# An attention, soft-mixture and feed-forward kernel: queries loaded with a token's heads side by side, and another order of work inside a step

## The chip, the core and the metric

The kernel runs on one core of a Trainium2 chip. Its engines work side by side, each through its own list of instructions in order: TensorE (PE) multiplies and transposes, VectorE (DVE) and ScalarE (ACT) do element-wise work and carry results out of the accumulator memory PSUM, GpSimd (POOL) works on SBUF alone, and SyncE (SP) issues the DMAs. The metric is the device time of one execution in microseconds (us).

## The reference

```
q_d, k_d, v_d = means of 4 neighbouring tokens of q, k, v
out = repeat(softmax(q_d k_d^T / 8) v_d, 4) + softmax(q k^T / 8 where |i - j| < 4) v
x = heads of out side by side                              # 2304 x 512
logits = x @ phi;  d = softmax over tokens;  c = softmax over slots
slot_out[e] = max((d.T @ x)[e] @ w1[e], 0) @ w2[e]         # 8 experts, 4 slots each
y = c @ slot_out                                           # 2304 x 512
result = max(y @ w_in, 0) ** 2 @ w_out                     # 512 -> 2048 -> 512
```

q, k and v are 4 batches x 8 heads x 576 tokens x 64 numbers in float32. w_in and w_out are float64; the kernel reads them as pairs of int32 and makes float32 of them on DVE ("narrow", L228 to L234, five turns over each piece).

## The kernel before

**Units and steps.** A batch and a pair of heads make a unit; there are 16. A written list, `START`, takes units 0 to 2 through their first stages. A loop over s = 3 to 15 then works through a string, `ORDER`, once per step; every letter is a stage, applied to unit s or to one that began one to five steps earlier, and a list `DRAIN` ends the attention. The scheduler is manual: an engine's instructions stand in the order of these letters.

Of unit s: `T` transposes the queries and `K` the keys (L404; ACT's L410 and L412 and DVE's L412 carry them out of PSUM into `q` and `kz`), `d` sums groups of four tokens on POOL into `qkd` (L420, L422), `Q` issues the loads of q and k of unit s+2 (L372). Of unit s-1: `S` local scores (L428, L434) with a maximum and a subtraction on DVE (L441, L442), `E` their exponential on ACT (L447), `s` coarse scores `sd` (L457), `m` their maximum, `e` their exponential `pd` (L468), `n`, `N` the sums and divisions (`pl` and `pd` on POOL), `L` the load of v (L389). Of s-2: `p` transposes the local probabilities (`ptp`, L495) and ACT copies them to `pt` (L496); `q` does that for the coarse ones (`pdp`, L507; `pdt`, L508). Of s-3: `V` multiplies with the values (`av`, L520), `x` and `X` make the coarse values (`vt`, `vdp`, `vd`). Of s-4: `D` multiplies the coarse ones (L549; ACT's `xd`, L554), `A` adds both (`xt`, L562), `t` transposes to tokens (`xp`, `xrp`; ACT's `xk`, `xr`) and forms the logits (L582). `h`, `H`, `g`, `G` are a batch's soft-mixture work; in the loop they fall in steps 8 and 12. `C` and `c` are narrowing turns, `l` issues weight loads.

**What sets when work can start.** All transposes, keys and queries included, share one PSUM tag `t` with three buffers: the fourth transpose in order waits until the first has been carried out. `pl`, `pt`, `qkd`, `xk` and `xr` have one buffer each; q, k, `kz`, `pdt` and `xt` have two. SP issues its DMAs in order; the eight landing semaphores are used in turn, so a DMA waits for the landing of the one issued eight before it. A plain step issues q, k, four pieces of v and two or three weight pieces.

**After the attention** come the soft-mixture's experts and then the feed-forward part, a loop of 80 hidden products (`up`, L1006), with the output products `po` (L1087) between them. The 2304 tokens come in five chunks. `SLOTS` says beside which of the hidden products the last pieces of the combine stand: `r1`, `r2`, `r3` make slices of a right factor (`arp`, L989; `rows`, L994 on ACT; `ast`, L996 on DVE) and `i2`, `i3` multiply w_in's last column blocks (`ap`, L979). `up`, `ap` and `arp` share one PSUM buffer.

Of the kernel before, what the change touches and what calls it, by code (L numbers as in the profile page):

```python
# [18 lines left out]
B, H, S, D = 4, 8, 576, 64  # L19
NP = H // 2  # L20
NU = B * NP
# [24 lines left out]
W32 = 5  # L46
LBE = 5
LOADN = [2, 2, 3] * 6
ORDER = "DTAhSEsmCHKQdgVxLepGtnXNqlc"
START = "T0 K0 phi L0 Q2 d0 f4 T1 S0 E0 s0 m0 K1 l2 Q3 d1 P e0 n0 N0 T2 S1 E1 s1 m1 K2 L1 Q4 l2 d2 e1 p0 n1 q0 N1 l2"  # L50
DDVE = (2,)
NDVE = (0,)
# [3 lines left out]
NRING = 28  # L56

LPOS = [0, 0, 0, 0, 8, 10, 12, 14, 67, 69, 70, 71, 74, 74, 77, 77]
SLOTS = {3: ['r1'], 11: ['i2'], 13: ['r2'], 19: ['i3'], 21: ['r3']}
NORDER = "w,w w,w w,w w,w o0,o1 o2 w,o3 o4,w o5,w w,o6 o7,w o8,w o9,w w,o10 o11,o12 o13,o14 o15"  # L60
NEXP = {(2, 0): 1, (6, 2): 1, (6, 3): 1, (7, 0): 1, (7, 1): 1}
WRES = 4
# [8 lines left out]
def attention_moe_ffn_kernel(  # L71
# [12 lines left out]
    nc = tc.nc  # L84
# [7 lines left out]
    def bank(tag, shape, bufs, name, dt=F32):  # L92
        return ps.tile(shape, dt, tag=tag, bufs=bufs, name=name)

    def bt(shape, name):
        return bank("t", shape, 3, name)
# [4 lines left out]
    ident = cp.tile([128, 128], F32, name="ident")  # L101
# [5 lines left out]
    for g in range(4):  # L107
        r = slice(32 * g, 32 * g + 32)
# [56 lines left out]
    def load_next(n=1):  # L165
        for _ in range(n):
            if not loads or not free:
                return
            kind, i, j = loads[0]

            fits = [x for x in free if x[0] is not wa or kind in ("w1", "w2") and i == 0 and int(x[1][1:]) >= WRES]
            fits.sort(key=lambda x: x[0] is not wa)
            if kind == "wout" or kind == "win" and (LPOS[4 * j + i] > 50 or lb is None) or kind != "win" and i == NE - 1:
                fits = [x for x in free if x[0] is ring]
            elif kind != "win" and i >= LBE + 1:
                fits = [x for x in fits if x[1][0] != "b"]
                fits.sort(key=lambda x: x[0] is ring)

            if any(j > 1 and (j, i // 2) not in win for k, i, j in got if k == "win") and kind != "win":
                if sum(x[0] is ring for x in free) < 2:  # L180
                    fits = [x for x in fits if x[0] is not ring]
            if not fits:
                return
            place = fits[0]
            free.remove(place)
            loads.popleft()
            load(kind, i, j, place)
# [109 lines left out]
    def narrow_next(n=1):  # L297
        for _ in range(n):
            narrow_turn()
# [10 lines left out]
    with tc.tile_pool(name="att", bufs=1, side="right") as ap:  # L310
        NV = 2
        vws, qs, kzs, pds, pdts, xts = [], [], [], [], [], []
        for i in range(2):
            t = aq.tile([128, SP + 6], F32, name=f"q{i}")
# [4 lines left out]
            t = aq.tile([128, 2, SP + 6], F32, name=f"kz{i}")  # L319
# [13 lines left out]
        for i in range(NV):  # L333

            t = ap.tile([128, NB, D], F32, name=f"vw{i}")
# [28 lines left out]
        def load_qk(u):  # L364
            b, hp = divmod(u, NP)
            h0 = 2 * hp
            st = U[u]
            for nm, src in (("q", q), ("k", k)):

                t = ring.tile([128, 1024], F32, tag=f"{nm}{u % 2}", name=f"{nm}{u}")[0:96, 0:768]  # L370
                t = t.rearrange("p (h c) -> p h c", h=2)
                nc.sync.dma_start(out=t, in_=src[b, h0:h0 + 2].rearrange("h (p r) d -> p h (r d)", r=6))  # L372
                st[nm] = t

        def load_v(u):
# [19 lines left out]

        def transposes(u, js=(0,)):
            st = U[u]
            for j in js:
                nm = "qk"[j]
                for h in range(2):  # L400

                    t = bt([128, 96, 3], f"tr{u}_{j}{h}")
                    for i in range(3):
                        nc.tensor.transpose(t[:, :, i], st[nm][:, h, 128 * i:128 * i + 128], ident[0:96, 0:96])  # L404
                    hr = slice(64 * h, 64 * h + 64)
                    to = (kzs[u % 2][hr, h] if j else qs[u % 2][hr])[:, 3:3 + S].rearrange("p (c r) -> p c r", r=2)
                    for r in range(2):
                        o, i_ = to[:, :, r], t[64 * r:64 * r + 64].rearrange("p c i -> p (c i)")
                        if not j:
                            nc.scalar.mul(out=o, in_=i_, mul=1.0 / 128.0)  # L410
                        else:
                            (nc.vector.tensor_copy if h else nc.scalar.copy)(out=o, in_=i_)  # L412

        def downsample(u):
            eng = nc.vector if u in DDVE else nc.gpsimd
# [264 lines left out]
        def gate_rows(b):  # L680
# [6 lines left out]
            else:  # L687
# [8 lines left out]
                nc.vector.tensor_tensor(out=ctt_lo, in0=m, in1=ctt_hi, op=ALU.subtract)  # L696

        load_qk(0)
        load_qk(1)
        la_scope = ExitStack()  # L700
        ok = lambda u: 0 <= u < NU
# [8 lines left out]
        def of_batch(x, b):  # L710
            if x == "h":
                stage_g1(b)
            elif x == "H":
                stage_eb(b)
                stage_g1b(b)
                keep_logits(b)
            else:
                (stage_g2 if x == "g" else stage_g3)(b)
# [19 lines left out]
        for s in range(3, NU):  # L738
            u1, u2, u3, u4, u5 = s - 1, s - 2, s - 3, s - 4, s - 5
            busy(FILL.get(s, FILLN))  # L740
            units = {
                "T": s, "K": s, "d": s, "Q": s + 2 if s else NU, "L": u1 if u3 >= 0 else NU,
                **dict.fromkeys("SEsmenN", u1), **dict.fromkeys("pq", u2), **dict.fromkeys("VxX", u3), **dict.fromkeys("DAt", u4),
            }
            for x in ORDER:
                if x in units:
                    if ok(units[x]):
                        step[x](units[x])
                elif x in "hHgG":
                    if last(u5):  # L750
                        of_batch(x, u5 // NP)
                elif x == "l":
                    if s >= 1:
                        load_next(LOADN[min(s, len(LOADN) - 1)])
                if x in "Cc":
                    narrow_next(CONV[s][x == "c"])
                if x == "K" and s >= NU - 2:
                    free.extend((ring, f"{y}{s % 2}") for y in "qk")
        for x in DRAIN.split():
            if x != "a":  # L760
# [15 lines left out]
        t = bt([1, 128], "mtp")  # L776
# [4 lines left out]
        t = bt([128, 2], "mbp")  # L781
# [23 lines left out]
        t = bt([128, 4, 32], "stp")  # L805
# [47 lines left out]
    for i in range(2):  # L853
        t = xp.tile([128, 2, 4, NS], F32, name=f"ht{i}")
# [216 lines left out]
    def ffn_down(c, f, between=()):  # L1071
        if f == 0 and c not in po:
            outs(c)
        nt = CHUNKS[c] // 128
        ghi, glo = gs_.pop((c, f))

        passes = [[(ghi, whi), (ghi, wlo)], [(glo, whi)]]
        if c == last_c and f == NF - 1:
            order = [(i, t) for i in range(nt) for t in passes]
        else:  # L1080
            order = [(i, t) for t in passes for i in range(nt)]
        for y, (i, terms) in enumerate(order):
            if y == 2:
                for x in between:
                    slots(x)
            for a, w in terms:
                nc.tensor.matmul(  # L1087
                    po[c][i], a[:, 128 * i:128 * i + 128], w[f],
                    start=(f == 0 and w is whi and a is ghi), stop=(f == NF - 1 and a is glo), skip_group_check=True,
                )  # L1090
        if f == NF - 1:
            for i in range(nt):
                o = fp.tile([128, DM], F32, tag="o", bufs=6, name=f"o{c}_{i}")
                r0 = c0s[c] + 128 * i
                if c == last_c and i == nt - 1:
                    half = DM // 2
                    nc.scalar.copy(out=o[:, 0:half], in_=po[c][i][:, 0:half])
                    nc.sync.dma_start(out=out[r0:r0 + 128, 0:half], in_=o[:, 0:half])
                    nc.vector.tensor_copy(o[:, half:], po[c][i][:, half:])
                    nc.scalar.dma_start(out=out[r0:r0 + 128, half:], in_=o[:, half:])  # L1100
                else:
                    (nc.scalar.copy if i % 2 else nc.vector.tensor_copy)(out=o, in_=po[c][i])
                    nc.sync.dma_start(out=out[r0:r0 + 128, :], in_=o)
# [4 lines left out]
    for i in range(2, len(steps) + LOOK):  # L1108
        if i < len(steps):
            c, f = steps[i]  # L1110
# [3 lines left out]
            k = NSTEPS[min(i - 2, len(NSTEPS) - 1)]  # L1114
# [38 lines left out]
```

## Time and profile before

| | |
|---|---|
| time, median of 3 runs | 442.85 us (442.78 to 445.08) |
| time of the profiled execution | 444.9 us |
| its span, first to last instruction | 443.2 us |
| steps 4 to 15 of the loop | 30.5 to 137.0 us |
| of them plain (ten) / with a batch's work (two) | 85.7 us / 20.8 us |
| PE busy over the whole span | 405.4 us (91%) |
| ACT / DVE / POOL busy over the span | 265.2 / 273.1 / 96.3 us |

A row of the timeline gives a start, a duration (for neighbouring instructions of one kind, their count and joint duration), the engine, the line, the tiles, and in brackets how long the engine had stood idle before it and what released it. A row of the windows gives for one stretch each engine's busy time, the clock granted to TensorE (1.00 is full speed), the busy share of the DMA engines and what they moved. Stages differ much, so a stage's own rows say what bounds it, not the shares over the span.

### The profile page before, as it was taken

What the parts mean: (1) busy time and instruction counts of PE and PEld (TensorE: products, weight loads), DVE (VectorE), ACT (ScalarE), POOL (GpSimd) and SP (SyncE); (2) the same over time, 40 slices, a digit from 0 to 9 for tenths busy, and PEclk for the clock granted to TensorE, in tenths of its full rate; (3) what the DMA queues carried; (4) which work ended last, traced back from release to release, by engine and by line L of the source; (5) the groups of instructions that cost most, each with busy time, mean ns of one, the idle gap of its engine ahead of it and who ended that gap; (6) DMA issues with size and microseconds to landing.
All of it is one profiled execution on the core that took longest, in us unless ns stands there. A gap on an engine that the chain in (4) does not pass through costs nothing.

```text
span 443.2 us, 10518 instructions
## 1 busy us (share of the span) xinstructions
PE 405.4 (91%) x4093; PEld 307.3 (69%) x4093; DVE 273.1 (62%) x606; ACT 265.2 (60%) x638; POOL 96.3 (22%) x169
## 2 busy tenths in 40 slices
PE   5698899889897889998899998999999999999996
PEld 4476675666775654554677786888888888888885
DVE  5858875876885631334889796955545554464442
ACT  5778787787876321244989796776444434444441
POOL 6576665674863200020000000000000000000000
PEclk9889999999999997999999999999999999999999
DMA  6999999999876997999980000002200100020002
GB/s 179 237 270 236 279 256 244 249 247 262 222 197 184 330 331 238 399 393 401 409 355 1 1 0 2 0 2 78 89 1 0 72 0 1 1 95 1 0 0 95
DMA packets 49387, 70.47 MB, mean 159 GB/s; under 512 B 24378, under 2 KB 30778, under 8 KB 49338
## 3 DMA queue, kind: packets, MB, share of 16 engines
q1 hardware_dynamic: 49194, 69.68, 52.3%
q8 instruction: 32, 0.52, 0.5%
q14 instruction: 17, 0.14, 0.1%
q10 hardware_dynamic: 144, 0.13, 0.1%
HBM read 65.07 MB, written 4.72 MB: 157 GB/s over the span
## 4 chain that ended last, share of the span: by engine, by line
PE 68%; DVE 11%; ACT 10%; DMA 6%; issue 3%; POOL 1%; SPq 0%; DVEq 0%; POOLq 0%; ACTq 0%
PE po L1087 40%; PE hp L863 4%; PE up L1006 4%; PE so L887 3%; ACT pd L468 3%; DMA q<-in_q_dram 2%; DMA wout<-in_moe_w_out_dram 2%; PE tr L404 2%; PE av L549 2%; PE s L434 2%; DMA win<-in_moe_w_in_dram 2%; DVE elp L442 2%; PE pdp L507 2%; ACT kz L412 2%; DVE mx L441 1%
## 5 line engine op out<-in xcount | busy, mean ns | idle before, releaser
L1087 PE MATMUL po<-wparts,gparts 128*128 128x512 f32 x864 | 211.7, 391 | 0.2 <-ACT r L1011 0.2
L1087 PEld LDWEIGHTS po<-wparts,gparts 128*128 128x128 f32 x864 | 161.4, 188 | 34.8 <-ACT r L1011 0.6
L1011 ACT ACTIVATE r<-up 128x384 f32<-128x384 f32 (+1 forms) x80 | 44.4, 555 | 77.8 <-PE up L1006 76.1
L1015 DVE TENSOR_TENSOR r<-r 128x512 f32<-128x512 f32 (+1 forms) x48 | 31.1, 648 | 58.8 <-ACT gparts L1014 58.8
L1019 DVE TENSOR_TENSOR gparts<-r,gparts 128x384 fp32r<-128x384 f32 (+1 forms) x78 | 49.8, 638 | 22.7 <-ACT gparts L1018 18.0
L1006 PE MATMUL up<-cst,ast 128*128 128x384 f32 (+1 forms) x80 | 30.2, 380 | 2.2 <-ACT rows L994 1.1
L481 POOL TENSOR_TENSOR pl<-elp,sm 64x350 f32<-64x350 f32 x30 | 27.4, 913 | 19.7 <-DVE sm L479 17.9
L410 ACT ACTIVATE q<-tr 64x288 f32<-64x288 f32 x64 | 27.8, 435 | 5.3 <-PE tr L404 4.5
L1014 ACT ACTIVATE gparts<-r 128x512 fp32r<-128x512 f32 (+1 forms) x50 | 29.8, 596 | 1.6
L420 POOL TENSOR_TENSOR s<-kz 64x288 f32<-64x288 f32 x30 | 20.1, 669 | 15.7 <-ACT kz L412 13.0
L562 DVE TENSOR_TENSOR xt<-av,xd 128x290 f32<-128x290 f32 x32 | 13.2, 453 | 10.9 <-ACT xd L554 10.7
L1006 PEld LDWEIGHTS up<-cst,ast 128*128 128x128 f32 x80 | 15.0, 188 | 6.6 <-ACT rows L994 1.9
L468 ACT ACTIVATE pd<-sd,mx 128x144 f32<-128x144 f32 x48 | 18.3, 381 | 1.4
L863 PE MATMUL hp<-w,sT 128*32 128x256 f32 x256 | 17.9, 432 | 0.4 <-DVE sT L810 0.4
L1017 ACT ACTIVATE r<-r 128x384 f32<-128x384 f32 (+1 forms) x30 | 17.4, 579 | 1.0
L404 PE MATMUL tr<-ident,q 96*128 96x96 f32 x96 | 13.0, 277 | 5.3 <-POOL maskf L202 4.1
L1018 ACT CAST gparts<-r 128x384 fp32r<-128x384 f32 (+1 forms) x30 | 17.0, 568 | 0.9
L457 PE MATMUL sd<-qkd 64*64 64x144 f32 x192 | 16.0, 301 | 1.3 <-POOL qkd L422 1.3
L508 ACT COPY pdt<-pdp 72x288 f32<-72x288 f32 x32 | 11.2, 396 | 9.3 <-PE pdp L507 9.3
L593 PE MATMUL xp<-ident,xt 128*128 128x128 f32 x64 | 10.2, 282 | 7.0 <-DVE kz L412 7.0
L887 PE MATMUL so<-w,ht 128*32 128x256 f32 x256 | 15.9, 382 | 0.8 <-issue 0.6
L488 POOL TENSOR_TENSOR pd<-pd,sm 128x432 f32<-128x432 f32 x16 | 15.5, 967 | 1.3
(190 smaller groups left out, 622.6 us busy)
## 6 DMA issues: line engine op xcount, KB each, us to landing
w<-in_moe_w_dram SPq DMA_DIRECT2D x64, 512.0 KB, 7.4
win<-in_moe_w_in_dram SPq DMA_DIRECT2D x16, 512.0 KB, 9.8
wout<-in_moe_w_out_dram SPq DMA_DIRECT2D x16, 512.0 KB, 10.2
vw<-in_v_dram SPq DMA_DIRECT2D x62, 80.0 KB, 6.5
q<-in_q_dram SPq DMA_DIRECT2D x16, 288.0 KB, 7.4
k<-in_k_dram SPq DMA_DIRECT2D x16, 288.0 KB, 7.8
out_dram<-o SPq DMA_DIRECT2D x17, 256.0 KB, 2.5
vw<-in_v_dram SPq DMA_DIRECT2D x2, 64.0 KB, 3.8
```

The source lines that it names most:

```text
L404: nc.tensor.transpose(t[:, :, i], st[nm][:, h, 128 * i:128 * i + 128], ident[0:96, 0:96])
L410: nc.scalar.mul(out=o, in_=i_, mul=1.0 / 128.0)
L468: nc.scalar.activation(out=pd[:, t], in_=sd[:, t], func=AF.Exp, bias=mx[:, 10 + t:11 + t], accum_out=ss[:, t:t + 1],)
L481: (nc.vector if u in NDVE else nc.gpsimd).tensor_tensor(out=pl[r, :, c0:c0 + W], in0=el[r], in1=sm[r, 0:NB].unsqueeze(2).to_broadcast([64, ...
L863: nc.tensor.matmul(t[32 * g:32 * g + 32], sT[:, kt], got["w1", e, kt][:, 256 * g:256 * g + 256], start=(kt == 0), stop=(kt == 3), tile_pos ...
L887: nc.tensor.matmul(so[32 * g:32 * g + 32], ht[:, g // 2, j], got["w2", e, j][:, g // 2, 256 * (g % 2):256 * (g % 2) + 256], start=(e == 0 ...
L1006: nc.tensor.matmul(t, ast[:, 128 * f:128 * f + 128], cst[:, c0s[c]:c0s[c] + n], start=True, stop=True)
L1011: nc.scalar.activation(out=r, in_=t, func=AF.Relu)
L1014: nc.scalar.activation(out=ghi, in_=r, func=AF.Square)
L1015: nc.vector.tensor_tensor(out=g, in0=r, in1=r, op=ALU.mult)
L1019: nc.vector.tensor_tensor(out=glo, in0=g, in1=ghi, op=ALU.subtract)
L1087: nc.tensor.matmul(po[c][i], a[:, 128 * i:128 * i + 128], w[f], start=(f == 0 and w is whi and a is ghi), stop=(f == NF - 1 and a is glo), ...
```

## The change

Three things change. (1) q of a unit comes by two DMAs instead of one: one per head, pieces of 256 bytes instead of 1536, so that in SBUF the two heads of a token lie side by side. Three 96 x 128 transposes then give 128 partitions holding both heads, and ACT's eviction of the queries is two instructions over 128 x 288 instead of four over 64 x 288. k is loaded and carried out as before. (2) `ORDER` is another string: the keys' transposes and S come first, D stands between S and the queries' transposes, q (the coarse probabilities) and V follow the coarse scores, and p comes near the end, behind t. The release of the last q and k buffers hangs on `T` instead of `K`. (3) In `SLOTS`, r1 moves from 3 to 5, i3 from 19 to 21 and r3 from 21 to 23.

```
-ORDER = "DTAhSEsmCHKQdgVxLepGtnXNqlc"
+ORDER = "hKSDHTQsAmgCEdqcVLGetxpnNXl"
-SLOTS = {3: ['r1'], 11: ['i2'], 13: ['r2'], 19: ['i3'], 21: ['r3']}
+SLOTS = {5: ['r1'], 11: ['i2'], 13: ['r2'], 21: ['i3'], 23: ['r3']}
...
-                t = t.rearrange("p (h c) -> p h c", h=2)
-                nc.sync.dma_start(out=t, in_=src[b, h0:h0 + 2].rearrange("h (p r) d -> p h (r d)", r=6))
+                if nm == "q":
+                    t = t.rearrange("p (r c) -> p r c", r=6)
+                    for h in range(2):
+                        nc.sync.dma_start(out=t[:, :, 64 * h:64 * h + 64], in_=src[b, h0 + h].rearrange("(p r) d -> p r d", r=6))
+                else:
+                    t = t.rearrange("p (h c) -> p h c", h=2)
+                    nc.sync.dma_start(out=t, in_=src[b, h0:h0 + 2].rearrange("h (p r) d -> p h (r d)", r=6))
...
+            if 0 in js:
+                for a in range(2):
+                    t = bt([128, 96, 3], f"tr{u}_0{a}")
+                    for i in range(3):
+                        nc.tensor.transpose(t[:, :, i], st["q"][:, 3 * a + i], ident[0:96, 0:96])
+                    to = qs[u % 2][:, 3:3 + S].rearrange("p (c r) -> p c r", r=6)[:, :, 3 * a:3 * a + 3]
+                    nc.scalar.mul(out=to, in_=t, mul=1.0 / 128.0)
...
-                if x == "K" and s >= NU - 2:
+                if x == "T" and s >= NU - 2:
```

On ACT, the step in which unit 11 begins stands so before; a name's number tells buffers apart, `tr_0` are queries and `tr_1` keys:

```order
L410 ACTIVATE q_135<-tr_00_1711 64x288 x2
L410 ACTIVATE q_135<-tr_01_1717 64x288 x2
L447 ACTIVATE elp<-elp 128x10x35
L412 COPY kz_138<-tr_10_1760 64x288 x2
L468 ACTIVATE pd_151,sd_1750<-sd_1750,mx_143 128x144 x3
L496 COPY pt<-ptp_0_1814 128x4x2x2x29
L496 COPY pt<-ptp_4_1820 128x2x2x29
L594 COPY xk<-xp_1823 128x4x128
L597 COPY xr<-xrp_1829 64x128
L508 COPY pdt_161<-pdp_0_1850 72x288
L508 COPY pdt_161<-pdp_1_1855 72x288
L554 ACTIVATE xd<-av_1_1784 128x288
```

And now, the same step on the same engine:

```order
L420 COPY kz_138<-tr_10_1697 64x288 x2
L562 ACTIVATE xd<-av_1_1627 128x288
L410 ACTIVATE q_135<-tr_00_1738 128x96x3
L410 ACTIVATE q_135<-tr_01_1743 128x96x3
L455 ACTIVATE elp<-elp 128x10x35
L516 COPY pdt_161<-pdp_0_1773 72x288
L516 COPY pdt_161<-pdp_1_1778 72x288
L476 ACTIVATE pd_151,sd_1753<-sd_1753,mx_143 128x144 x3
L602 COPY xk<-xp_1812 128x4x128
L605 COPY xr<-xrp_1818 64x128
L504 COPY pt<-ptp_0_1831 128x4x2x2x29
L504 COPY pt<-ptp_4_1837 128x2x2x29
```

The keys' copies and `xd` open the step, the queries take two instructions for four, `pdt` has gone ahead of `pd`, and `pt` has gone from the middle to the end.

On PE the end of a step before, from the local probabilities' transposes on:

```order
L495 MATMUL ptp_0_1814<-ident,pl 128x128 x4
L495 MATMUL ptp_4_1820<-ident,pl 128x128
L593 MATMUL xp_1823<-ident,xt_163 128x128 x4
L596 MATMUL xrp_1829<-ident,xt_163 64x128
L582 MATMUL lgt<-xt_163,phis 32x128 x4
L582 MATMUL lgt<-xt_163,phis 32x16 x4
L539 MATMUL vdp_1845<-ident,vt 72x128 x2
L507 MATMUL pdp_0_1850<-ident,pd_152 72x112 x3
L507 MATMUL pdp_1_1855<-ident,pd_152 72x112 x3
L549 MATMUL av_1_1784<-pdt_160,vd 64x144 x4
L404 MATMUL tr_00_1871<-ident,q_1611 128x96 x3
```

And now:

```order
L601 MATMUL xp_1812<-ident,xt_163 128x128 x4
L604 MATMUL xrp_1818<-ident,xt_163 64x128
L590 MATMUL lgt<-xt_163,phis 32x128 x4
L590 MATMUL lgt<-xt_163,phis 32x16 x4
L503 MATMUL ptp_0_1831<-ident,pl 128x128 x4
L503 MATMUL ptp_4_1837<-ident,pl 128x128
L547 MATMUL vdp_1846<-ident,vt 72x128 x2
L416 MATMUL tr_10_1865<-ident,k_1591 128x96 x3
L416 MATMUL tr_11_1871<-ident,k_1591 128x96 x3
```

`ptp` stands behind `xp`, `xrp` and the logits; `pdp` has left this place (it follows the coarse scores now), and `av` with `vd` comes behind the next step's keys and local scores.

On DVE in the feed-forward part, near the hidden product of block 12, now (`w_13`, `w_14`: pieces of w_out being narrowed; `ast`: the slice r3):

```order
L1027 TENSOR_TENSOR gparts_3464<-r_11_4145,gparts_3464 128x512
L232 TENSOR_SCALAR w_13_4041<-w_13_4041 128x512
L232 TENSOR_SCALAR w_14_4043<-w_14_4043 128x512
L233 SCALAR_TENSOR_TENSOR w_13_4041<-wout_0_3397,w_13_4041 128x512
L233 SCALAR_TENSOR_TENSOR w_14_4043<-wout_0_3399,w_14_4043 128x512
L1004 TENSOR_TENSOR ast<-rows_4158,ast 64x512
L1027 TENSOR_TENSOR gparts_3461<-r_12_4177,gparts_3461 128x384
```

Before, the `ast` subtraction stood ahead of the two 384- and 512-wide `gparts` of block 11, so it has moved behind these two and three pairs of narrowing turns (L231, L232 and L233 of `w_13` and `w_14`).

## Rows read from the trace of the kernel before

**Rows 1.** Cores: span and mean granted clock.

```profile
core 0: 443.2 us, clock 0.983
```

**Rows 2.** Windows: stretch, us, busy of PE PEld DVE ACT POOL, PEclk, DMA share, GB/s.

```profile
30.50:64.60 34.10, 30.00 (x594) 23.72 (x593) 26.63 (x64) 27.41 (x81) 23.33 (x34) 1.00 1.12 254
64.60:75.40 10.80, 9.87 (x159) 6.38 (x158) 6.89 (x21) 7.55 (x25) 4.26 (x7) 1.00 1.06 233
75.40:101.50 26.10, 22.96 (x445) 17.85 (x446) 20.04 (x49) 20.70 (x61) 18.79 (x27) 1.00 1.05 246
101.50:111.50 10.00, 9.51 (x159) 6.17 (x158) 7.10 (x22) 7.66 (x26) 4.10 (x7) 1.00 1.10 278
111.50:137.00 25.50, 22.48 (x442) 17.58 (x442) 20.28 (x49) 20.50 (x61) 18.69 (x27) 1.00 0.74 205
84.00:92.70 8.70, 7.45 (x148) 5.67 (x146) 7.76 (x18) 6.78 (x20) 5.13 (x8) 1.00 1.13 245
```

**Rows 3.** Timeline of PE, step of unit 11.

```profile
92.65 0.71 PE L404 MATMUL tr<-ident,q 96*128 96x96 f32 x6
...
97.90 0.63 PE L593 MATMUL xp<-ident,xt 128*128 128x128 f32 x4 [0.62 <-DVE kz L412]
98.86 0.30 PE L596 MATMUL xrp<-ident,xt 128*64 128x128 f32 x1 [0.33 <-ACT pt L496]
...
101.15 0.63 PE L404 MATMUL tr<-ident,q 96*128 96x96 f32 x5
```

**Rows 4.** Timeline of ACT, the same step.

```profile
93.15 1.79 ACT L410 ACTIVATE q<-tr 64x288 f32<-64x288 f32 x4
...
96.03 0.88 ACT L412 COPY kz<-tr 64x288 f32<-64x288 f32 x2
...
98.21 0.74 ACT L496 COPY pt<-ptp 128x464 f32<-128x464 f32 x2
98.84 0.61 ACT L594 COPY xk<-xp 128x512 f32<-128x512 f32 x1
```

**Rows 5.** Timeline of PE where the loop starts (step 3).

```profile
21.36 1.19 PE L404 MATMUL tr<-ident,q 96*128 96x96 f32 x6 [0.92 <-DMA q<-in_q_dram]
```

**Rows 6.** Timeline of SP ahead of that: issues of k3 and of four pieces of v.

```profile
11.59 0.33 SPq L372 DMA_DIRECT2D k<-in_k_dram  x1
12.01 4.04 SPq L389 DMA_DIRECT2D vw<-in_v_dram  x4
```

**Rows 7.** DMA issues at 11.5 to 11.9: KB, us to landing.

```profile
k<-in_k_dram SPq DMA_DIRECT2D x1, 288.0 KB, 10.6
```

**Rows 8.** DMA issues at 15.5 to 16.0, the last piece of v.

```profile
vw<-in_v_dram SPq DMA_DIRECT2D x1, 80.0 KB, 7.9
```

**Rows 9.** Timeline of SP: issues of k6, k8 and k9.

```profile
35.44 0.33 SPq L372 DMA_DIRECT2D k<-in_k_dram  x1
...
52.49 0.33 SPq L372 DMA_DIRECT2D k<-in_k_dram  x1
...
60.84 0.33 SPq L372 DMA_DIRECT2D k<-in_k_dram  x1
```

**Rows 10.** DMA issues at 52.4 to 52.6.

```profile
k<-in_k_dram SPq DMA_DIRECT2D x1, 288.0 KB, 8.3
```

**Rows 11.** DMA packets at 34.4 to 41.3.

```profile
DMA packets 1642, 1.77 MB, mean 257 GB/s; under 512 B 1068, under 2 KB 1402, under 8 KB 1639
```

**Rows 12.** DMA packets at 51.5 to 57.

```profile
DMA packets 724, 1.74 MB, mean 316 GB/s; under 512 B 165, under 2 KB 393, under 8 KB 723
```

**Rows 13.** Feed-forward part: timeline of PE.

```profile
222.64 0.45 PE L1006 MATMUL up<-cst,ast 128*128 128x384 f32 x1 [0.52 <-ACT rows L994]
...
268.96 0.42 PE L979 MATMUL ap<-win,soT 128*32 128x128 f32 x8 [1.98 <-DVE win L234]
...
282.65 0.34 PE L1006 MATMUL up<-cst,ast 128*128 128x384 f32 x1
```

**Rows 14.** Timeline of DVE, beside the last of these rows.

```profile
283.62 1.29 DVE L233 SCALAR_TENSOR_TENSOR w<-wout,w 128x512 int32<-128x512 int32 x2
```

More of the change, by code (lines that the diff above doesn't have):

```diff
@@ L397, in transposes @@
             st = U[u]
-            for j in js:
-                nm = "qk"[j]
+            if 0 in js:
[5 more added lines that the diff above has]
+                    nc.scalar.mul(out=to, in_=t, mul=1.0 / 128.0)
+            if 1 in js:
                 for h in range(2):
-                    t = bt([128, 96, 3], f"tr{u}_{j}{h}")
+                    t = bt([128, 96, 3], f"tr{u}_1{h}")
                     for i in range(3):
-                        nc.tensor.transpose(t[:, :, i], st[nm][:, h, 128 * i:128 * i + 128], ident[0:96, 0:96])
+                        nc.tensor.transpose(t[:, :, i], st["k"][:, h, 128 * i:128 * i + 128], ident[0:96, 0:96])
                     hr = slice(64 * h, 64 * h + 64)
-                    to = (kzs[u % 2][hr, h] if j else qs[u % 2][hr])[:, 3:3 + S].rearrange("p (c r) -> p c r", r=2)
+                    to = kzs[u % 2][hr, h][:, 3:3 + S].rearrange("p (c r) -> p c r", r=2)
                     for r in range(2):
[L408 to L412, printed above, removed]
+                        (nc.vector.tensor_copy if h else nc.scalar.copy)(out=to[:, :, r], in_=t[64 * r:64 * r + 64].rearrange("p c i -> p (c i)"))
         def downsample(u):
```

## The prediction

> **What bounds the kernel now.** I read the cores first: one core, 443.2 us at a clock of 0.983 [rows 1], so nothing is throttled for long. Then the windows by steps of the attention loop, since the new order and the new query path lie there. The reader is to see the ten plain steps in the first, third and fifth window of [rows 2]: 34.1 + 26.1 + 25.5 = 85.7 us with PE busy 30.00 + 22.96 + 22.48 = 75.44 us. PE, at full clock, is idle 10.26 us, 1.03 per step; ACT is busy 68.61 us, so 6.9 of a step's 8.57. No engine is full. The two batch steps last 20.8 us with PE busy 19.38. Third, the timeline of PE in one step [rows 3]: from one set of query transposes to the next are 8.50 us, with two waits, 0.62 ahead of `xp` for DVE's copy of `kz` and 0.33 ahead of `xrp` for ACT's `pt`. Both are the PSUM tag with three buffers: `xp` takes the buffer of the keys' second half, `xrp` that of the first four `ptp`. Outside them PE works 7.55 us. Fourth, ACT in that step [rows 4]: the queries' 1.79 us stand first, so the exponential and the keys' 0.88 end only around 96.9, and `pd`, `pt` and `xk` follow back to back. The step is pinned by evictions that reach PE late, not by PE's work.
>
> **The new step.** Queries: six transposes before and after, evictions four of 1.79 / 4 = 0.45 us before, two after. No row shows 128 x 288 with groups of three; its price lies between 0.45 (a 64-partition one of the same 288 columns, were partitions free) and 0.90 (two of them). I take 0.45: `xk` moves 512 columns over 128 partitions in 0.61. ACT loses 0.9 us per step, and at the other end nothing. The removed 0.9 stands beside PE's work, so by itself it is worth nothing; it decides whether the evictions keep up. Order: tag `t` is now taken by keys, queries, `pdp`, `xp`, `xrp`, `ptp`, `vdp`. `xp` takes the buffer of the queries' second half, carried out some 2 us before; `xrp` and the first `ptp` those of `pdp`. So both waits of [rows 3] lose their cause, worth 0.95. What is late next: the last `ptp` takes `xp`'s buffer and needs `xk` (0.61, behind `pd` on ACT), and the next step's keys take the first `ptp`'s and need half of `pt`'s 0.74 [rows 4]. Between `xp`'s end and the last `ptp` PE has `xrp`, the logits and four transposes; between `ptp` and the next keys only the two `vdp`. I leave 0.1 each. A plain step is then 7.55 + 0.2 = 7.75.
>
> DVE is the cover that could give out: in the step with two narrowing turns it is busy 7.76 of 8.70 [rows 2]. Packed into 7.75 it would be full, so I give two such steps 0.3 more. Eight steps of 7.75 and two of 8.05 are 78.1; I keep 78.5 for what the layout does not see, so 85.7 - 78.5 = -7.2. The batch steps' PE idles 20.8 - 19.38 = 1.4 us; half of it goes, -0.7. Bounds for the stage: all idle gone, -10.26 - 1.4 = -11.7; other hand-offs take the place of the old, 0 (the coarse `av` now stands on PE between S and the queries' transposes, and `xd` ahead of the queries on ACT, so a late `pdt` would hold both). I take -7.9.
>
> After the attention the weights' loads run on buffers that the experts free, and nothing there waits for a fixed time, so I carry the gain through one to one.
>
> **The start.** Step 3 waits for q3, which lands just before 21.36 [rows 5]. The keys now go first, and k3 is issued at 11.59 and takes 10.6 [rows 6, 7]: 22.2, so 0.8 later at least. On PE everything of step 3 stands behind it, and ACT and DVE wait for that. Each q that is issued ahead of it has a second half now; one piece of v takes SP at most 4.04 / 4 = 1.0 us there, waits between them included, against 0.33 for k [rows 6]. Four more halves (units 0 to 3) would put back k3 by 0 (they hide in waits for landings) to 4 x 1.0 us. I take 1.2 on top of 0.8: +2.0, with bounds 0.8 and 4.8.
>
> **Loads.** k6 is issued at 35.44 and k9 at 60.84 [rows 9]: 25.40 / 3 = 8.47 us per unit, whether the steps want it or not, and a 7.75 step will want it sooner. k8 is issued at 52.49, lands 8.3 later at 60.8 [rows 9, 10] and is wanted by a keys-first step 8 at 64.6 [rows 2], after the change at 64.6 + 2.0 - 4 x 0.8 = 63.4: a cushion of 2.6. From step 8 to step 12 the work takes 10.05 + 3 x 7.75 = 33.3 and the loads 4 x 8.47 = 33.9, so 2.0 are left. If a unit's loads become slower by p, unit 12 is nine units on from unit 3 and late by 9p - 2.0. What p is, no row shows; bounds from two views. Low: k3 (288 KB in pieces of 1536 bytes) lands at 22.2, at most 1.0 us after q3 was there, 3.5 ns per KB; the last of four pieces of v (320 KB in pieces of 256) is issued at 12.01 + 4.04 - 0.60, with 0.60 for an issue in itself, an estimate between k's 0.33 and 1.0, and lands 7.9 later at 23.35 [rows 6, 8], 1.15 us after k3: 3.6 ns per KB. So p = 0.03 and small pieces cost nothing. High: 1068 of 1642 packets are small in one stretch and 257 GB/s are moved, 165 of 724 in another with 316 [rows 11, 12]. At 316 GB/s the first one's 1.77 MB would take 5.6 us instead of 6.9: 1.3 us for 900 more small packets, 1.44 ns each, and a split q has 2 x 96 x 6 = 1152: p = 1.66. So the lateness is between 0 and 9 x 1.66 - 2.0 = 12.9. I take p = 0.33, nearer to the landing rows, as they are a piece of the same kind on the same queue: +1.0.
>
> A rule speaks against this part. The Trainium skill's page "DMA: Bandwidth & Descriptors" says under "Why small descriptors are slow (HBM only)" that on trn2 a 256-byte descriptor pays three cycles on eight, and longer ones the same three once. The landing rows of v do not agree with it, the two stretches go its way. By it the 1152 descriptors cost 12,672 cycles against 192 x 51 = 9,792, 29% more, an estimate from that page; on 1.0 us for such a load p would be 0.3 and the lateness 0.7, so the sum would come out 0.3 lower.
>
> **Feed-forward part.** The wait of 1.98 ahead of i3's products for DVE's narrowing [rows 13] goes, since two blocks later the piece is ready; the 0.52 that `up` waits behind r1 for `rows` goes too. r3 now stands on DVE behind the L233 pair that ends at 283.62 + 1.29 = 284.9 [rows 14], and needs some 0.65 itself (half of that pair): 285.55. The `up` that reads it is due at 282.65 [rows 13] and eight products of r3 later: at 0.42 for eight such [rows 13] or double that, 283.1 to 283.5. A new wait of 2.05 to 2.5; I take 2.05. Sum -0.45, so -0.4, with bounds -2.5 (PE has other products to put in) and 0.
>
> **Sum.** -7.9 + 2.0 + 1.0 - 0.4 = -5.3 on the profiled execution's 444.9: 439.6. That execution is 2.05 above the median of the runs shown; the same difference on 442.85 gives 437.5.
>
> **Rivals.** (A) As worked out, 437.5, own range 434.5 to 440.6. (B) The step stays pinned near 8.4 by another hand-off: `pt`, now last on ACT, and `xk` behind `pd` hold the keys that open the next step. For it: every term of PE's order waits on the same three buffers as before. Against it: ACT has 0.9 us less. Ten steps gain 1.7, batch steps nothing: -1.7 + 2.0 - 0.4 = -0.1, 442.75; loads are never late then. (C) The loads become the bound, and it gets slower: by p = 1.66 from the packets, -6.3 + 12.9 = +6.6, 449.5. By the eight landing semaphores another way leads there: k6 to k9 is 8.47 us for some 8.25 DMAs, 1.03 each, and one more per unit gives p = 1.03, +7.3 - 6.3 = +1.0, 443.9. The two together say about 447. It decides from 9p - 2.0 = 6.3 on, p = 0.92. For it: the stage's DMA share is above 1.0 up to step 12 [rows 2]; against it: the landings of v. (D) The loads keep up and the start costs only its 0.8, and no engine keeps a residue: 85.7 - 75.5 = 10.2, - 0.7, + 0.8, - 0.4: -10.5, 432.4.
>
> **Chances.** A 0.50, B 0.18, C 0.18, D 0.14. About 0.5% of 442.85, 2.2 us, is what a measurement of this kernel can tell from no change: faster is below 440.6, slower above 445.1. A lies nearly all in faster (0.47 of 0.50), D all of it, B nearly all in same, C 0.15 in slower and 0.03 in same. So faster 0.62, same 0.22, slower 0.16. The range leaves out half of D and most of C's upper half: 432.5 to 446.5.
>
> **What would show it.** In the profile after: plain steps of 7.7 to 8.0 between keys' transposes, with no wait above 0.2 ahead of `xp` or `xrp`; query evictions of 128 x 288 at about 0.45 each, two per unit; step 3 opening at 22.2 to 24 behind k3; no wait for a q or k load over 1 us in steps 4 to 12; i3 without a wait, and a wait of about 2 us ahead of the `up` of block 12 behind r3. I am wrong if PE waits for k in several steps (C), if PE's idle time per plain step stays above 0.8 with loads in time (B), or if the new query eviction costs 0.9.

## The result, and the profile after

The changed kernel takes 442.21 us (median of 20 runs, 439.83 to 447.26). In the same comparison the kernel before has a median of 446.0 over 20 runs, more than the 442.85 of the three that were shown. The ratio is 0.9918 with an interval of 0.989 to 0.9947: 0.8% faster, 0.5 to 1.1%. The forecast, 437.5 against 442.85, was a ratio of 0.988. The sign was right, the size too large. Executions of one kernel spread over 7 to 10 us with the granted clock, so the ratios, here and below, are of fast executions alone.

The profiled execution of the changed kernel took 442.17 us; its cores' row, beside [rows 1]:

```profile
core 0: 440.4 us, clock 0.985
```

Its span is 2.8 us shorter. The windows (columns as in [rows 2]) show a step with one narrowing turn, one with two, step 14, and the part of step 14 at half clock:

```profile
90.10:97.70 7.60, 7.37 (x150) 5.79 (x148) 6.55 (x19) 5.59 (x18) 5.86 (x9) 1.00 1.12 283
45.20:54.10 8.90, 7.34 (x150) 5.84 (x148) 8.44 (x19) 5.69 (x18) 6.30 (x8) 1.00 1.07 263
116.80:127.40 10.60, 10.28 (x150) 7.97 (x148) 7.84 (x21) 5.86 (x18) 5.78 (x9) 0.68 0.49 133
117.80:124.40 6.60, 6.60 (x84) 5.05 (x80) 3.96 (x9) 2.61 (x7) 3.91 (x6) 0.50 0.55 170
```

The first step is what was forecast, even a little better: 7.6 us with PE busy 7.37. In the second PE has no more work, yet it takes 8.9, and DVE is busy 8.44 of it. In the third TensorE was granted half of its speed (1.2 GHz) for 6.6 us. The same step takes 7.83 in a second profile of the same kernel in which it ran at full clock (shown below), so the stretch cost 2.8 us of the 10.64.

PE in the good step, to be held against [rows 3]:

```profile
90.10 0.66 PE L416 MATMUL tr<-ident,k 96*128 96x96 f32 x6
...
95.28 0.66 PE L601 MATMUL xp<-ident,xt 128*128 128x128 f32 x4
95.77 0.27 PE L604 MATMUL xrp<-ident,xt 128*64 128x128 f32 x1
...
97.68 0.71 PE L416 MATMUL tr<-ident,k 96*128 96x96 f32 x6 [0.23 <-ACT pt L504]
```

Both old waits, 0.62 ahead of `xp` and 0.33 ahead of `xrp`, are gone; what is left is 0.23 ahead of the next keys, for `pt`. ACT in the same step, against [rows 4]:

```profile
92.73 0.80 ACT L410 ACTIVATE q<-tr 128x288 f32<-128x288 f32 x2
...
96.18 0.63 ACT L602 COPY xk<-xp 128x512 f32<-128x512 f32 x1
...
97.07 0.71 ACT L504 COPY pt<-ptp 128x464 f32<-128x464 f32 x2
```

The queries leave PSUM in 0.80 us instead of 1.79: 0.40 each, a little under the low end of the bounds (0.45).

Now the step with two turns: DVE, GpSimd, and PE at its end.

```profile
48.97 0.61 DVE L469 TENSOR_REDUCE mx<-sd 128x3 f32<-128x432 f32 x1 [0.23 <-PE sd L465]
49.49 2.01 DVE L233 SCALAR_TENSOR_TENSOR win<-win,win 128x512 int32<-128x512 int32 x2
51.42 1.99 DVE L234 SCALAR_TENSOR_TENSOR win<-win,win 128x512 int32<-128x512 int32 x2
53.33 0.36 DVE L538 COPY vt<-av 128x75 f32<-128x75 f32 x2
```

```profile
49.96 2.07 POOL L428 TENSOR_TENSOR s<-kz 64x288 f32<-64x288 f32 x2
```

```profile
53.84 0.42 PE L547 MATMUL vdp<-ident,vt 128*72 128x128 f32 x2 [1.56 <-DVE vt L538]
```

In the new string both turns, `C` and `c`, stand between `m` and `x`; before, `c` was the last letter. So the copy of `vt` waits for four us of narrowing, and `vdp`, with all of PE's list behind it, for `vt`. Such waits stand at the ends of steps 6, 9, 10 and 13: 1.56, 1.02, 1.03 and 1.56, together 5.17 us. Steps 5 and 14 have two turns as well, but of the kinds L228 to L232 that read one input; a pair of these takes 1.2 to 1.5 us, and `vdp` does not wait for `vt` there. Each of the four that wait holds an L233 or L234.

The length of a step, from one bias product of the local scores (L428, L436 after the change) to the next, in this and in later profiles (steps 8 and 12 hold a batch's work; step 14 of the second row and step 4 of the third hold half clock):

| step | 4 | 5 | 6 | 7 | 8 | 9 | 10 | 11 | 12 | 13 | 14 |
|---|---|---|---|---|---|---|---|---|---|---|---|
| before | 8.42 | 8.44 | 8.52 | 8.45 | 11.04 | 8.45 | 8.89 | 8.51 | 10.28 | 8.52 | 8.44 |
| after | 8.32 | 7.83 | 9.00 | 8.62 | 9.89 | 8.36 | 9.03 | 7.63 | 10.17 | 8.89 | 10.64 |
| order, old queries | 10.96 | 8.12 | 8.64 | 8.14 | 10.23 | 8.13 | 8.27 | 8.14 | 11.02 | 8.64 | 8.13 |
| queries, old order | 8.31 | 8.32 | 8.37 | 8.77 | 10.62 | 8.31 | 8.38 | 8.30 | 10.61 | 8.47 | 8.32 |
| c behind x | 7.63 | 7.63 | 7.63 | 9.49 | 10.91 | 7.63 | 7.72 | 8.75 | 9.89 | 7.63 | 8.14 |
| c last, p behind V | 9.45 | 8.78 | 8.49 | 8.68 | 9.61 | 8.67 | 8.68 | 8.49 | 9.67 | 8.67 | 8.68 |

The start, against [rows 5 to 7]: PE, SP, and the DMA's time to landing.

```profile
21.39 0.69 PE L416 MATMUL tr<-ident,k 96*128 96x96 f32 x6
```

```profile
13.47 0.92 SPq L377 DMA_DIRECT2D k<-in_k_dram  x1
```

```profile
k<-in_k_dram SPq DMA_DIRECT2D x1, 288.0 KB, 7.8
```

Step 3 opens as early as before and waits for nothing: k3 is issued 1.9 us later than before but lands 7.8 after its issue, at 21.3, where 22.2 was its time before. In the loop one wait for a load is left, at step 5:

```profile
37.34 0.69 PE L416 MATMUL tr<-ident,k 96*128 96x96 f32 x6 [0.95 <-DMA k<-in_k_dram]
```

Experts and feed-forward part, against [rows 13]:

```profile
204.05 0.64 PE L895 MATMUL so<-w,ht 128*32 128x256 f32 x8 [0.28 <-DMA w<-in_moe_w_dram]
...
268.53 1.08 PE L987 MATMUL ap<-win,soT 128*32 128x128 f32 x32
...
279.81 0.41 PE L1014 MATMUL up<-cst,ast 128*128 128x384 f32 x1 [1.72 <-DVE ast L1004]
```

i3's wait of 1.98 is gone, the new wait behind r3 is 1.72, and the last expert now waits 0.28 for a weight piece.

### The profile page after: what moved, and what is told of

The parts are those of the page before. It is cut to its first block, busy times and chain, and to the rows that moved or that the text cites. A ratio compares the mean times of both kernels' runs of the same rounds, so it can differ in the third digit from the quotient of the medians.

```text
span 440.4 us, 10445 instructions
## 1 busy us (share of the span) xinstructions
PE 406.2 (92%) x4093; PEld 309.2 (70%) x4093; DVE 279.2 (63%) x606; ACT 248.1 (56%) x606; POOL 96.1 (22%) x169
## 4 chain that ended last, share of the span: by engine, by line
PE 74%; ACT 8%; DVE 8%; DMA 5%; issue 3%; POOL 1%; SPq 1%; POOLq 0%; DVEq 0%; ACTq 0%
PE po L1095 40%; PE hp L871 4%; PE up L1014 3%; PE so L895 3%; PE sd L465 3%; PE tr L408 2%; PE s L442 2%; DMA k<-in_k_dram 2%; DMA win<-in_moe_w_in_dram 2%; PE av L557 2%; DVE win L234 2%; PE tr L416 2%; PE av L528 2%; PE pdp L515 1%; DVE win L233 1%
## 5 line engine op out<-in xcount | busy, mean ns | idle before, releaser
L489 POOL TENSOR_TENSOR pl<-elp,sm 64x350 f32<-64x350 f32 x30 | 23.1, 772 | 29.1 <-DVE sm L487 14.8
L428 POOL TENSOR_TENSOR s<-kz 64x288 f32<-64x288 f32 x30 | 23.2, 772 | 3.0 <-ACT kz L420 0.8
L420 ACT COPY kz<-tr 64x288 f32<-64x288 f32 x32 | 13.6, 424 | 9.5 <-PE tr L416 9.2
L420 DVE COPY kz<-tr 64x288 f32<-64x288 f32 x32 | 14.6, 458 | 6.4 <-PE tr L416 5.9
L410 ACT ACTIVATE q<-tr 128x288 f32<-128x288 f32 x32 | 13.4, 468 | 6.9 <-PE tr L408 6.9
L871 PE MATMUL hp<-w,sT 128*32 128x256 f32 x256 | 16.6, 407 | 0.4 <-DVE sT L818 0.4
L408 PEld LDWEIGHTS tr<-ident,q 96*128 96x128 f32 x96 | 10.3, 161 | 9.0 <-POOL maskf L202 5.3
## 6 DMA issues: line engine op xcount, KB each, us to landing
wout<-in_moe_w_out_dram SPq DMA_DIRECT2D x16, 512.0 KB, 10.2
```

The lines of the kernel that those rows point to most:

```text
L408: nc.tensor.transpose(t[:, :, i], st["q"][:, 3 * a + i], ident[0:96, 0:96])
L420: (nc.vector.tensor_copy if h else nc.scalar.copy)(out=to[:, :, r], in_=t[64 * r:64 * r + 64].rearrange("p c i -> p (c i)"))
L428: eng.tensor_tensor(out=s1[r], in0=t[:, :, 0], in1=t[:, :, 1], op=ALU.add)
L871: nc.tensor.matmul(t[32 * g:32 * g + 32], sT[:, kt], got["w1", e, kt][:, 256 * g:256 * g + 256], start=(kt == 0), stop=(kt == 3), tile_pos ...
```

## The experiments

**The order and the slots with the queries' old path.**

```
 ORDER, SLOTS, release at "T": as after the change
 load_qk, transposes: as before
```

> The new order of letters and the new slots, but q loaded by one DMA and carried out by four ACT instructions over 64 x 288, as before. Theory 1 (order and lighter eviction need each other): ACT's 1.79 us for the queries put pd, xk and pt back by 0.9 us in every step, and the next step's keys wait for pt; plain steps 8.4 to 8.8 us, wait ahead of the keys' transposes 0.8 or more, ratio to before 0.996 to 1.000 (what the slots give, 1.0 us). Theory 2 (the order alone takes the waits away): plain steps with one narrowing turn 7.6 to 7.9 us as after the whole change, ratio 0.990 to 0.993.

Ratio 0.9956 (0.9916 to 0.9997), nearer to the first theory's; most plain steps 8.1 to 8.3 us, between the two. The wait is not where theory 1 had it: the keys wait at most 0.5 for `pt`, and in most steps not at all; the last `ptp` waits for `xk`. PE and ACT in step 11:

```profile
98.28 0.33 PE L495 MATMUL ptp<-ident,pl 128*128 128x128 f32 x1 [0.56 <-ACT xk L594]
```

```profile
93.42 1.77 ACT L410 ACTIVATE q<-tr 64x288 f32<-64x288 f32 x4
```

The 1.77 us put `xk` back, and the last `ptp` needs `xp`'s buffer. Of the 0.88 us that the whole change takes from step 11 (8.51 to 7.63), the order alone gives 0.37. (Step 4, 10.96, holds an idle of 1.62 us that nothing in the profile explains, and half clock.)

**The queries' path alone.**

```
 ORDER, SLOTS, release at "K": as before
 load_qk, transposes: as after the change
```

> The new query load and eviction alone, old order, old slots. Theory 1: the step stays pinned by the chain maximum, exponential, kz, pd, pt; query evictions 0.8 instead of 1.79 us per step but steps 8.4 to 8.6, ratio 0.998 to 1.002. Theory 2 (small pieces slow the loads): q and k land late, PE waits for them in some steps, ratio 1.005 or more. Theory 3 (ACT's work is the bound): steps 0.5 or more shorter, ratio 0.988 or less.

Ratio 0.9951 (0.9913 to 0.999), a little below theory 1's, though the interval reaches into it; steps 8.3, between theories 1 and 3. No step waits for a load, which goes against theory 2. The profile's rows of the DMA queue (packets, MB, the sum of the packets' time as a share of 16 engines' span), before and here, agree: a third more packets, and no more time in all.

```profile
q1 hardware_dynamic: 49194, 69.68, 52.3%
...
q1 hardware_dynamic: 64810, 69.68, 52.1%
```

The old waits stay, the first a little shorter (0.47 for 0.62):

```profile
95.94 0.63 PE L601 MATMUL xp<-ident,xt 128*128 128x128 f32 x4 [0.47 <-DVE kz L420]
96.91 0.30 PE L604 MATMUL xrp<-ident,xt 128*64 128x128 f32 x1 [0.35 <-ACT pt L504]
```

So 0.21 in step 11 from the queries alone, 0.37 from the order, 0.88 from both: together they give more than their sum. The ratios of the whole kernel are too wide to show that by themselves.

**The slots alone.**

```
-SLOTS = {3: ['r1'], 11: ['i2'], 13: ['r2'], 19: ['i3'], 21: ['r3']}
+SLOTS = {5: ['r1'], 11: ['i2'], 13: ['r2'], 21: ['i3'], 23: ['r3']}
```

> The three slots alone. The wait of 1.98 us ahead of i3's products and the 0.52 behind r1 go, a wait of 1.7 us ahead of the hidden product behind r3 comes: 1.0 us less in the feed-forward part, ratio 0.997 to 0.998. If the slots only move the wait, 0.5 us or less.

Ratio 0.9954; its interval (0.992 to 0.9987) holds the expected 0.997 to 0.998 and can't say more. In the profile the stretch from the first hidden product to the end is 231.24 us against 232.2 before and 231.2 after the whole change: 1.0 us, as expected.

**The second narrowing turn at the step's end.**

```
-ORDER = "hKSDHTQsAmgCEdqcVLGetxpnNXl"
+ORDER = "hKSDHTQsAmgCEdqVLGetxpnNXlc"
```

> The changed kernel with the second narrowing turn (c) at the end of the step's order instead of ahead of G, e, t and x. Theory 1 (DVE: both turns stand ahead of the copy of vt in six steps, and vdp waits 1.0 to 1.6 us for it in four): those waits go, steps 6, 9, 10 and 13 come to 7.6 to 8.1 us, 3 to 5 us less than the changed kernel, ratio to before 0.981 to 0.986. Theory 2 (DVE is full in these steps anyway, and the turn now holds the next step's copy of kz and the maximum of s): a wait of 0.5 to 1.5 us ahead of the queries' transposes or the coarse scores takes its place, ratio 0.990 to 0.993 as after. Theory 3 (the clock): half clock for some 6.7 us between 117 and 125 us comes with the new order; it stands here too, and the ratio stays above 0.988.

Ratio 0.9873 (0.9811 to 0.9935), above the expected 0.981 to 0.986, though the interval reaches into it. No `vdp` waits for `vt` any more, and steps 6, 9 and 13 take 7.63, 7.65 and 7.73 instead of 9.00, 8.36 and 8.89 (step 10: 10.75, with half clock at 84.9 to 88.3 and, ahead of it, an idle of 1.2 us that nothing in the profile explains). So theory 1 holds for the steps, and theory 3's half clock at 117 to 125 us is not there. Behind the attention a part of the gain is given back in this profile: from the first expert's product to the first hidden product 45.5 us, where the changed kernel took 43.2. A small part of that is a wait of PE:

```profile
202.53 0.64 PE L895 MATMUL so<-w,ht 128*32 128x256 f32 x8 [0.70 <-DMA w<-in_moe_w_dram]
```

The wait for the last expert's weights was 0 before, 0.28 after the change, and 0.70 here. Most of the rest goes with half clock at 204.3 to 207.7 us, where the other profiles have full clock.

**The second turn behind x.**

```
-ORDER = "hKSDHTQsAmgCEdqcVLGetxpnNXl"
+ORDER = "hKSDHTQsAmgCEdqVLGetxcpnNXl"
```

> The changed kernel with the second narrowing turn directly behind the copy of vt (x) instead of ahead of it. Theory 1 (vt late): vdp waits no more, as with the turn at the end; but the sums sm and the copy of vd now stand behind the turn, so the division pl starts some 1.3 to 2 us later and the last stage ptp or av with vd may wait 0 to 0.5 us. Plain steps 7.6 to 8.1 us, ratio to before 0.982 to 0.989. Theory 2 (what costs is a turn running beside GpSimd's sums: 1.3 us alone, 2.0 us beside them): the second turn takes 1.3 us here, as GpSimd's sums of the keys are over by then. If DVE's fullness were the cause, the steps with two turns would stay at 8.4 to 9.0 us.

Ratio 0.9833 (0.9774 to 0.9891), beside 0.9905 of the changed kernel in the same comparison (below); the intervals overlap. Span of the profiled execution 435.5. Steps 4, 5, 6, 9 and 13 take 7.63. The turn itself takes 1.70 in step 6 and not 1.3: GpSimd's last sum still runs. That steps with two turns come to 7.63 rules out that DVE is simply full in them. PE at the beginning of steps 6, 8 and 12:

```profile
44.36 0.71 PE L416 MATMUL tr<-ident,k 96*128 96x96 f32 x6 [0.23 <-ACT pt L504]
...
61.51 0.69 PE L416 MATMUL tr<-ident,k 96*128 96x96 f32 x6 [1.62 <-DMA k<-in_k_dram]
...
96.51 0.69 PE L416 MATMUL tr<-ident,k 96*128 96x96 f32 x6 [1.38 <-DMA k<-in_k_dram]
```

What is late next is the loads, 3.0 us in two places. No run shows whether the split q has a share in that, since none has steps of 7.63 us with the old load.

**Other slots, with the turn at the end.**

```
-SLOTS = {5: ['r1'], 11: ['i2'], 13: ['r2'], 21: ['i3'], 23: ['r3']}
+SLOTS = {5: ['r1'], 11: ['i2'], 13: ['r2'], 20: ['i3'], 22: ['r3']}
```

> The second turn at the end of the step, and i3 and r3 beside hidden products 20 and 22 instead of 21 and 23. If the wait of 1.7 us behind r3 comes from the two L233 turns that stand ahead of its subtraction on DVE, it goes or halves here, and i3, two products' time later than 19, waits 0 to 1 us: 0.7 to 1.7 us less in the feed-forward part than with 21 and 23, ratio to before 0.980 to 0.986. If every place meets turns on DVE, a wait of 1 to 2 us stays and the ratio equals that of the turn at the end alone.

Ratio 0.9829 (0.978 to 0.9879), not to be told from the turn at the end alone. i3 does not wait, and behind r3 the wait is for ACT, no longer for DVE:

```profile
272.06 0.50 PE L1014 MATMUL up<-cst,ast 128*128 128x512 f32 x1 [0.94 <-ACT rows L1002]
```

In the profile the feed-forward part takes 230.2 us, 1.0 less than with 21 and 23.

**The turn at the end, and p directly behind V.**

```
-ORDER = "hKSDHTQsAmgCEdqVLGetxpnNXlc"
+ORDER = "hKSDHTQsAmgCEdqVpLGetxnNXlc"
```

> The second turn at the end of the step, and the local probabilities' transposes (p) directly behind V as before, not behind t. Theory 1 (the three PSUM buffers make the order): xp then takes the buffer of pdp's second half and xrp that of the first four ptp, whose copy stands on ACT behind pd; a wait of 0.3 to 0.8 us ahead of xrp comes back, and the keys no longer wait for pt: plain steps 7.8 to 8.3 us against 7.65, ratio 0.988 to 0.993. Theory 2 (the keys' place and the lighter eviction alone do it, p's place is indifferent): 7.6 to 7.7 us, ratio as with the turn at the end alone.

Ratio 0.9975 (0.9938 to 1.0012), steps 8.5 to 8.8. Theory 1 holds in kind, worse than expected and in another place. PE at the beginning of step 7:

```profile
57.74 0.71 PE L416 MATMUL tr<-ident,k 96*128 96x96 f32 x6 [0.89 <-ACT xk L602]
```

With `ptp` ahead of `xp` the next keys take `xp`'s buffer, and `xk` stands on ACT behind `pd` and `pt`. p's place is worth the whole gain of the steps.

**The changed kernel again.**

```
 (unchanged)
```

> The changed kernel once more, for a second profile beside the variants. If the half clock at 117 to 125 us belongs to the change, it stands at the same place; if clock drops fall anywhere, it stands elsewhere or not at all, step 14 takes 7.5 to 7.9 us (two turns, of the kinds that cost 1.2 and 1.5), and the waits of vdp for vt in steps 6, 9, 10 and 13 are there again with 1.0 to 1.6 us each. Ratio to before 0.989 to 0.995.

Ratio 0.9905 (0.9866 to 0.9944). The profiled execution took 447.35 us at a mean granted clock of 0.969. In it the waits of `vdp` are the same, to 0.01 us: 1.56, 1.02, 1.03, 1.56; steps 6 and 13 take 8.91 and 8.90, step 14 only 7.83. PE in step 6:

```profile
53.60 0.41 PE L547 MATMUL vdp<-ident,vt 128*72 128x128 f32 x2 [1.56 <-DVE vt L538]
```

And the bias products that bound step 14 here:

```profile
122.09 0.31 PE L436 MATMUL s<-maskb,identb 128*128 128x350 bf16 x1
...
129.92 0.31 PE L436 MATMUL s<-maskb,identb 128*128 128x350 bf16 x1
```

Half clock is granted at 63 to 74 and 145 to 152 here, not at 117 to 125. So the stretch in step 14 is not fixed to a place of the change. One more stretch, at the first expert, is in every profile with one of two lengths, some 3.4 or some 6.8 us. The expert's products before, after, and here:

```profile
166.92 6.33 PE L863 MATMUL hp<-w,sT 128*32 128x256 f32 x64 [0.38 <-DVE sT L810]
...
166.00 4.98 PE L871 MATMUL hp<-w,sT 128*32 128x256 f32 x64 [0.38 <-DVE sT L818]
...
170.31 6.41 PE L871 MATMUL hp<-w,sT 128*32 128x256 f32 x64 [0.38 <-DVE sT L818]
```

The same changed kernel takes 4.98 in one execution and 6.41 in the other.

**Both mended places together; and k ahead of q.** The first has c behind x and the slots 20 and 22; the second in addition:

```
-            for nm, src in (("q", q), ("k", k)):
+            for nm, src in ((("q", q), ("k", k)) if u < 3 else (("k", k), ("q", q))):
```

> Both mended places together: the second turn behind x, i3 and r3 beside products 20 and 22. If the two add up: plain steps 7.63 us as with the turn behind x, feed-forward part 230.2 us from its first hidden product as with 20 and 22 against 231.2, ratio to before 0.978 to 0.985. Loads: one or two waits of 1 to 2 us for k ahead of the keys' transposes stay.

> The same, and from unit 3 on k is loaded ahead of the two halves of q. Theory 1 (loads bind where the step is 7.63 us, and the keys, wanted first, land last): k lands some 1.5 us sooner, q some 1.2 later, which the queries' transposes 2 us on in the step do not notice; the waits of 1.4 to 1.6 us for k go or fall under 0.5, 1 to 3 us less, ratio 0.973 to 0.982. Theory 2 (the stream as a whole is late, whatever its order): the wait goes over to the queries' transposes or to a later step, ratio as without.

The first: 0.9824 (0.9763 to 0.9885), as expected, the lowest ratio of all, though not to be told from those of the two that it joins. The second: 0.9897 (0.9834 to 0.9961), theory 1 is wrong. The waits for k did not go but became 2.11, 2.08 and 2.95 us (steps 7, 8 and 11; mean granted clock 0.969 in this execution), the last one here:

```profile
91.22 1.19 PE L416 MATMUL tr<-ident,k 96*128 96x96 f32 x6 [2.95 <-DMA k<-in_k_dram]
```

That the stream of loads as a whole is late at steps of 7.63 us, theory 2, fits better, but theory 2 did not foresee longer waits; why it is later with k first was not found out.

**The sums of units 6 and 13 on DVE.**

```
-DDVE = (2,)
+DDVE = (2, 6, 13)
```

> The changed kernel with the sums of four tokens of units 6 and 13 on DVE instead of GpSimd, so that in steps 6 and 13 the two narrowing turns run with GpSimd idle; one look. Theory 1 (a turn costs more beside GpSimd's sums): the pairs of L233 and L234 in steps 6 and 13 take 1.3 to 1.45 us each instead of 2.0, while those of steps 9 and 10, unchanged, still take 2.0. Theory 2 (2.0 us is what a turn costs in this place, for its own data or what stands ahead of it): 2.0 us in all four. The steps 6 and 13 themselves become longer, as DVE has the sums too (some 2 us of them).

One execution, 439.67 us, beside 445.61 of the kernel before: too few for a ratio. DVE in step 6 and in step 9:

```profile
49.74 1.28 DVE L233 SCALAR_TENSOR_TENSOR win<-win,win 128x512 int32<-128x512 int32 x2
...
52.95 1.29 DVE L234 SCALAR_TENSOR_TENSOR win<-win,win 128x512 int32<-128x512 int32 x2
...
78.71 1.98 DVE L233 SCALAR_TENSOR_TENSOR win<-win,win 128x512 int32<-128x512 int32 x2
```

And GpSimd, idle from 48.6 to 55.4 us:

```profile
55.44 1.62 POOL L489 TENSOR_TENSOR pl<-elp,sm 64x350 f32<-64x350 f32 x2 [6.87 <-DVE sm L487]
```

Theory 1: with GpSimd idle the same turns take 1.28 and 1.29 instead of 2.01 and 1.99 (step 13: 1.28 and 1.29 for 2.01 and 1.98), and 1.98 to 2.01 where GpSimd works as before. `vdp` waits 2.14 in these two steps, as DVE has the sums too.

## Why the prediction was right in sign and too large

From the starts of the bias products the change of 2.8 us in the two profiles splits so, each with its forecast behind it:

| stretch | before, us | after, us | change | forecast |
|---|---|---|---|---|
| opening of step 3 | 22.3 | 21.9 | -0.4 | +2.0 |
| step 3 itself | 8.66 | 7.64 | -1.0 | none |
| steps 4 to 15 | 105.8 | 106.4 | +0.5 | -7.9 + 1.0 |
| from there to the first hidden product | 74.1 | 73.3 | -0.9 | 0 |
| feed-forward part | 232.2 | 231.2 | -1.0 | -0.4 |

The miss is in steps 4 to 15, 7.4 us: 4.6 by the step that failed (the second point below), 2.8 by half clock in step 14. The start and step 3 gave 3.4 us more than forecast, the first expert 0.9 and the feed-forward part 0.6. That the total came as near as -2.8 to -5.3 is in part luck.

- **The waits of [rows 3] lose their cause, 0.95 per step:** right. They are gone, step 11 takes 7.63 for a forecast 7.75, and the batch steps lost 1.26 together (11.04 + 10.28 to 9.89 + 10.17) where 0.7 was said.
- **"In the step with two narrowing turns DVE ... two such steps 0.3 more":** this step failed. There are six such steps (5, 6, 9, 10, 13, 14, as `CONV` says), not two, and a busy sum of 7.76 did not tell the price: both turns stand ahead of `vt` in the new list, beside GpSimd's sums of the keys, and the L233 and L234 among them take up to 2.0 us for the 1.28 that one takes alone. 0.6 us was allowed; 5.17 us of waits came, in four steps. Moving one letter takes these waits away (c at the end, c behind x). I had laid out PE and ACT of the new step, but not DVE's row by row.
- **Rivals:** by its numbers B came closer than A. The nine plain steps outside step 14 last 75.4 us together, 8.4 each, and PE is idle 0.9 in each on the mean, above the 0.8 that was to speak for B. But the hand-off is not B's: the keys wait at most 0.5 for `pt`, and 5.17 of the 8.2 us that PE is idle there are `vdp` waiting for `vt`.
- **Clock:** the prediction took full clock in the loop. This execution lost 2.8 us to half clock in step 14. It is not a term of the change alone: it stands elsewhere in the second profile, and one such stretch (29 to 33 us) is there with the slots alone, whose loop is the old one.
- **Start +2.0:** wrong, it was -0.4. The 0.8 for waiting on k3 and the 1.2 for later issues did not come; k3 landed 1.0 earlier, though the split q's halves of 144 KB stand ahead of it.
- **Loads +1.0:** right in size, by luck: one wait of 0.95. It stands at step 5, and in the second profile of the same kernel no step of the loop waits for a load; the forecast let a lateness of p = 0.33 per unit build up to step 12. No run shows such a p: with the queries' path alone no step waits, and the packets take no more time in all. At steps of 7.63 us the loads cost 3.0. Rival C's cause thus stands next, but did not decide.
- **"The gain carries through one to one":** right as far as the profiles show. Up to the first expert both take the same 30.1 us from the last bias product. The 0.9 behind it is not the change's: the first expert's 64 products took 4.98 us for 6.33 at another granted clock (from 165 to 175 us 0.66 and 1.00 in the two halves, 0.56 and 0.76 before), and 6.41 in the second profile of the changed kernel. The last expert's wait for weights, 0.28 here and 0.70 with the turn at the end, does not simply follow a faster loop: with the turn behind x the first expert starts earlier still, and nothing waits for these weights.
- **Feed-forward part -0.4:** mechanism right, each wait where it was put; -1.0, since the new wait was 1.72 and not 2.05, and the waits around r1 gave 0.26 more.

Without the 2.8 us of half clock, steps 4 to 15 gained 2.3 where 7.9 less 1.0 was forecast; the 4.6 between them match the 5.17 us of waits less the 0.6 allowed. With the second turn behind x, in a loop all at full clock, steps 4 to 15 gain 4.7 (105.8 to 101.1) with 3.0 us of load waits in them: without these it would be 7.7, the size forecast for the stage.

## What to carry to other kernels

When an order is changed for the sake of one engine pair, lay out every in-order engine's list for a step, fillers included: a filler that stood last and now stands ahead of a small copy makes its whole length a wait for the engine behind that copy. Take a filler's duration from rows where the same neighbours run beside it, since the same pair of instructions took 1.28 or 2.01 us. Once one stage is packed, look at what is next to bind (here the loads in the loop). Before a difference between two profiles is put down to a change, compare the granted clock of the same stretch in both, and in a second profile of the same kernel: here a stretch of half clock was worth 2.8 us one way and another 0.9 the other way.

## What had not been expected of the hardware

DVE's narrowing instruction and GpSimd's sums slow each other: L233's pair takes 1.28 alone and 2.01 beside them, the two sums of keys 1.40 to 1.46 in most steps before and 2.07 beside it. The Trainium skill's "GPSIMD Engine Reference", "1. Specifications", says that GpSimd's interfaces to SBUF are shared with VectorE, with contention where DVE reads two SBUF inputs, as L233 does, or runs in a 2-port perf mode; for L233 the rows agree. A pair of one-input turns, 0.75 to 0.92 in most steps before, takes 1.45 to 1.48 beside the sums as well; no run here shows in which mode these run.

Which of the two engines pays differs. Before the change the last turn of step 6 ran beside GpSimd's divisions, and GpSimd paid, 2.64 for the 1.62 that they take alone, while DVE's pair took 1.28:

```profile
54.98 1.28 DVE L234 SCALAR_TENSOR_TENSOR win<-win,win 128x512 int32<-128x512 int32 x2
```

```profile
54.26 2.64 POOL L481 TENSOR_TENSOR pl<-elp,sm 64x350 f32<-64x350 f32 x2
```

So the 1.28 of the old place was no price for the new one. What decides who pays was not tested.

TensorE was granted half of its speed in the middle of a busy loop. In the loops of seven profiles (the changed kernel twice; order alone, slots alone, c at the end, both mended places, k first) such a stretch came during an idle of PE of 1.1 to 2.95 us or up to 2 us after it, and lasted 3.4 to 10.2 us. But other idles of that length (1.56 in step 6, 2.14 with the sums on DVE, 2.11 with k first) were not followed by one, so a long idle is not enough; what decides was not settled.
